# Converting float64 weights on chip: a whole-number significand times a power of two made by ScalarE, five VectorE operations per piece in place of six

## The chip, the cores and the metric

The kernel runs on one core of a Trainium2 chip. The time is the device time of one execution in microseconds (us), the median of several runs. A core has a matrix engine (TensorE, in the profile PE, with its weight loads as PEld), a vector engine (VectorE, DVE), a scalar engine for functions and copies (ScalarE, ACT), a general one (GpSimd, POOL) and one that mostly issues transfers (SyncE, SP). Each has its own instruction stream; they meet at semaphores.

## What is computed

```python
# attention part: q, k, v are (4, 8, 768, 64) float32
for t in range(S):
    state = gamma[None, :, None, None] * state + np.einsum('bhd,bhe->bhde', k[:, :, t], v[:, :, t])
    y[:, :, t] = scale * np.einsum('bhd,bhde->bhe', q[:, :, t], state)
x = y.transpose(0, 2, 1, 3).reshape(B * S, H * D)        # (3072, 512)
# feed-forward part: w_in (512, 2048), w_out (2048, 512)
h = x @ w_in
sp = np.maximum(h, 0.0) + np.log1p(np.exp(-np.abs(h)))
g = h * erf(sp)
return (g @ w_out).astype(np.float32)                    # (3072, 512)
```

The two weight matrices come out of the set-up as float64 (a float32 array times a float64 scalar). The kernel reads them as 64-bit words and makes float32 of them on the chip. This conversion is what is changed.

## The kernel before

The recurrence is done in 24 blocks of 128 positions (`j`), each with transposes, a masked product of q and k, a product with v and a running state. Blocks 0 to 3 feed the first 512 rows (groups `g` = 0 to 3, plain products); the later rows use a scheme of seven products of half size, which needs sums of weight quarters.

The weights come in 16 pieces of 1 MiB (two transfers of 512 KB each). A piece is 128 partitions by 1024 numbers of two 32-bit words, `lo` and `hi`. It lands in one of four spare areas of the weight tiles `w_in_sb` and `w_out_sb`; further spare areas hold intermediate results (`low`, and `tops`, of which there are two, used in turn).

```python
spare = [
    x[:, s, 4:7].rearrange("p a b c -> p (a b c)") for s, x in
    ((0, w_out_sb), (1, w_out_sb), (1, w_in_sb), (0, w_in_sb))
]
raws = [x[:, : 2 * CE].bitcast(I64) for x in spare]        # place 2 lies in w_in_sb
low = spare[0][:, 2 * CE :].bitcast(U32)
tops = [x[:, 2 * CE :].bitcast(U32) for x in spare[1:3]]
pieces = [("in", 0), ("in", 1)]                            # then in 2, in 3, out 0, out 1, in 4, ...
place = [n % 4 if n < n_p - 4 else (n - n_p + 4) % 3 for n in range(n_p)]

def conversion(n):                                         # L192 on; cut
    nc.vector.tensor_scalar(top, hi, 3, 0x3FFFFFF8, ...)             # L205: 8 times the magnitude bits
    yield
    nc.vector.scalar_tensor_tensor(top, hi, 0xC0000000, top, ...)    # L209: sign and top bit back
    yield
    nc.scalar.activation(square, square, AF.Square)                  # L213, in place on hi
    yield
    nc.vector.tensor_scalar(low, top, 0xFF800000, None, ...)         # L215: power of two of it
    yield
    nc.vector.scalar_tensor_tensor(lowf, lo, 2.0**-52, lowf, ...)    # L217: low word, scaled
    yield
    nc.vector.tensor_tensor(lowf, topf, lowf, op=ALU.add)            # L219
    yield
    nc.vector.scalar_tensor_tensor(to, square..., F64_LEAST**2, lowf..., op0=ALU.is_ge, op1=ALU.mult)  # L221
    done.add(pieces[n])
    load_pieces_after(n)      # load the next piece of this place
    yield
```

Each engine runs its instructions in the order in which the program emits them. The steps of the conversion are woven in between other work: `pace(x)` adds `x` to a budget and emits one step of `weights()` for every whole unit of it; `need(what)` emits steps until a piece is there.

```python
def weights():                                             # L250
    for n in range(2):
        for i, _ in enumerate(conversion(n)):
            if i != 2:
                yield
    before = iter(())
    for n in range(2, n_p):
        now = conversion(n)
        for _ in range(2):
            next(now)
            yield
        if n > 2:
            next(before)
            yield
        next(now)
        for _ in before:
            yield
        before = now
        ...

def ret_scale(j):       # VectorE, L397: k and q of a block times their decays
    nc.vector.tensor_tensor(KQ[j], KQ[j], by, op=ALU.mult)
    pace(-1.1)
def ret_transpose(j):   # TensorE L412, then ScalarE copies kT and qT, L418
    ...
    pace(1)
def ret_scores(j):      # TensorE L425
    ...
    pace(1)
def ret_mask(j):        # VectorE L437, two per block: am = scores times mask
    ...
    pace(-1.2)
def ret_out(j):         # TensorE L460, L465 (needs am), L474; ScalarE copies xT, L479
    ...
    pace(2.5)
def ret_loads(j):
    if j == 0 or j == JPC:
        load(j + 3)                                        # k, q, v of a block
    if j in (1, 2):
        load_piece(j + 1)

for j in range(n_first):                                   # blocks 0 to 3
    S_(j); M(j); K_(j + 1); O_(j); T(j + 1)                # scores, mask, scale, out, transpose (cut)
    ret_loads(j)
    pace(1)
    A(j)                                                   # state, VectorE L493/L495
```

After that come, for each group, `hidden` (products with w_in, TensorE L541, copied to `h` by ScalarE, L544), `gate` (Softplus and Erf on ScalarE, L506 and L511), `gated` (two products on VectorE, L530) and `project` (products with w_out, L554); from group 4 on `hidden_part` (L611) and `project_part` (L683). `load_pieces_after` holds the loads back until block 3 is emitted.

Of the kernel before, what the change touches and what calls it, by code (L numbers as in the profile page):

```python
# [12 lines left out]
F32 = mybir.dt.float32  # L13
U32 = mybir.dt.uint32
I64 = mybir.dt.int64
AF = mybir.ActivationFunctionType
ALU = mybir.AluOpType
PSUM = bass.MemoryType.PSUM

P = 128  # L20
# [18 lines left out]
}  # L39


F64_LEAST = float(np.array(897 << 20, np.uint32).view(np.float32))


@with_exitstack
def kernel(
# [13 lines left out]
    nc = tc.nc  # L60
# [14 lines left out]
    const = ctx.enter_context(tc.tile_pool(name="const", bufs=1))  # L75
# [52 lines left out]
    def w_out_of(ft):  # L128
# [5 lines left out]
    CE = 2 * d_model  # L134
    spare = [
        x[:, s, 4:7].rearrange("p a b c -> p (a b c)") for s, x in
        ((0, w_out_sb), (1, w_out_sb), (1, w_in_sb), (0, w_in_sb))
    ]
    raws = [x[:, : 2 * CE].bitcast(I64) for x in spare]
    low = spare[0][:, 2 * CE :].bitcast(U32)  # L140
    tops = [x[:, 2 * CE :].bitcast(U32) for x in spare[1:3]]
    pieces = [("in", 0), ("in", 1)]
    for n in range(4):
        if n < 3:
# [2 lines left out]
    n_p = len(pieces)  # L147
# [3 lines left out]
    def load_piece(n):  # L151
        which, i = pieces[n]
        w = raws[place[n]]
        if which == "in":
            for r in range(2):
                nc.sync.dma_start(
                    w[r * D : (r + 1) * D].rearrange("p (g f) -> p g f", g=n_k),
                    w_in[r * DH : (r + 1) * DH, i * 2 * P : (i + 1) * 2 * P].rearrange(
                        "(g p) f -> p g f", p=D
                    ),  # L160
                )
        else:
            for d in range(2):
                nc.sync.dma_start(
                    w.rearrange("p (d f c) -> p d f c", d=2, f=2)[:, d],
                    w_out[i * 2 * P : (i + 1) * 2 * P, d * DH : (d + 1) * DH].rearrange(
                        "(f p) c -> p f c", p=P
                    ),
                )
# [18 lines left out]
    def conversion(n):  # L188

        which, i = pieces[n]  # L192
        words = raws[place[n]].bitcast(U32).rearrange("p (n w) -> p n w", w=2)
        lo, hi = words[:, :, 0], words[:, :, 1]
        square = hi.bitcast(F32)
        half, s, at = i // 4, i % 4 // 2, i % 2
        if which == "in":
            to = w_in_sb[:, s, 2 * half : 2 * half + 2, :, at * 2 * P : (at + 1) * 2 * P]
            form, sizes = "p (d k f) -> p d k f", dict(d=2, k=2)
        else:  # L200
            to = w_out_sb[:, s, 2 * half : 2 * half + 2, at * 2 : at * 2 + 2, :]
            form, sizes = "p (d f c) -> p d f c", dict(d=2, f=2)
        top = tops[n % 2]
        topf, lowf = top.bitcast(F32), low.bitcast(F32)
        nc.vector.tensor_scalar(  # L205
            top, hi, 3, 0x3FFFFFF8, op0=ALU.logical_shift_left, op1=ALU.bitwise_and
        )
        yield
        nc.vector.scalar_tensor_tensor(  # L209
            top, hi, 0xC0000000, top, op0=ALU.bitwise_and, op1=ALU.bitwise_or  # L210
        )
        yield
        nc.scalar.activation(square, square, AF.Square)  # L213
        yield
        nc.vector.tensor_scalar(low, top, 0xFF800000, None, op0=ALU.bitwise_and)  # L215
        yield
        nc.vector.scalar_tensor_tensor(lowf, lo, 2.0**-52, lowf, op0=ALU.mult, op1=ALU.mult)  # L217
        yield
        nc.vector.tensor_tensor(lowf, topf, lowf, op=ALU.add)  # L219
        yield  # L220
        nc.vector.scalar_tensor_tensor(  # L221
            to,
            square.rearrange(form, **sizes),
            F64_LEAST**2,
            lowf.rearrange(form, **sizes),
            op0=ALU.is_ge,
            op1=ALU.mult,
        )
        done.add(pieces[n])
        load_pieces_after(n)  # L230
        yield

    def sums(which, s):

        if which == "in":
            assert all(("hidden", 2 * FG + s * FG + u) in done for u in range(FG))
            x = {name: w_in_sb[:, s, at] for name, at in IN.items()}
            of = (("S1", "21", "22", 1), ("S2", "S1", "11", 0), ("S3", "11", "21", 0), ("S4", "12", "S2", 0))
        else:
            assert ("project", s) in done  # L240
            x = {name: w_out_sb[:, s, at] for name, at in OUT.items()}
            of = (("T1", "12", "11", 0), ("T2", "22", "T1", 0), ("T3", "22", "12", 0), ("T4", "21", "T2", 0))
        for to, a, b, plus in of:
            nc.vector.tensor_tensor(x[to], x[a], x[b], op=ALU.add if plus else ALU.subtract)
            yield
        done.add(("sums " + which, s))
# [3 lines left out]
    def weights():  # L250


        for n in range(2):
            for i, _ in enumerate(conversion(n)):
                if i != 2:
                    yield
        before = iter(())
        for n in range(2, n_p):
            now = conversion(n)
            for _ in range(2):  # L260
                next(now)
                yield
            if n > 2:
                next(before)
                yield
            next(now)
            for _ in before:
                yield
            before = now
            if pieces[n - 1] == ("out", 5):  # L270
                yield from sums("in", 0)
        yield from before

    def later_sums():
        for which, n in (("in", 1), ("out", 0), ("out", 1)):
            yield from sums(which, n)

    weight_steps = weights()
    last_steps = later_sums()
    room = 0.0  # L280
# [9 lines left out]
    def need(*what):  # L290
        nonlocal room
        while what not in done:
            if next(weight_steps, done) is done:
                next(last_steps)
            room -= 1

    ident = const.tile([P, P], F32, name="ident")
    make_identity(nc, ident)
    nc.scalar.dma_start(d_k, decay_k)
# [3 lines left out]
    for s in range(2):  # L303
# [9 lines left out]
        out=causal, in_=causal, compare_op=ALU.is_ge, fill=0.0,  # L313
# [607 lines left out]
```

## Time and profile before

| what | value |
|---|---|
| time, median of 3 runs | 714.78 us (713.53 to 715.28) |
| span of the profiled execution | 711.6 us |
| TensorE busy | 697.9 us, 98% |
| VectorE busy | 399.4 us, 56%, 548 instructions |
| ScalarE busy | 257.0 us, 36%, 289 instructions |
| HBM read, written | 39.86 MB, 6.29 MB |
| chain of work that ended last | TensorE 95%, ScalarE 2%, DMA 2%, VectorE 1% |

A line of the profile in order of time has the start, the duration, the engine, the source line (L205 is line 205 of the kernel), the operation and its output and inputs by tile, and in brackets the idle time before it with what ended it. The source lines of the kernel after differ from those of the kernel before, as some lines are gone. Busy time of an engine is no measure of what it costs: only what the chain of waits runs through sets the end. The groups of the conversion in the kernel before, by line (count, busy time, mean duration), summed over tiles:

| line | engine | count | mean |
|---|---|---|---|
| L205, L215 | VectorE, one source | 16 each | 0.69 us |
| L209, L217, L219, L221 | VectorE, two sources | 16 each | 1.22 to 1.23 us |
| L213 | ScalarE, Square | 16 | 1.17 us |

### The profile page before, as it was taken

The page shows a single profiled execution, that of the slowest core. Times are in us where ns is not written, and L with a number is a line of the kernel's source. Part 1 is how long each engine was busy: PE and PEld are TensorE (multiplying, and loading weights), DVE is VectorE, ACT ScalarE, POOL GpSimd, SP SyncE. Part 2 cuts the span into 40 slices and gives each one's busy share as a digit, 9 for nine tenths or more (in the row PEclk, how much of TensorE's full clock was granted, in tenths as well). Part 3 has the DMA queues.
Part 4 walks back from the last instruction along what each step waited for, and adds up shares of the span by engine and source line. Part 5 has one row for each costly group of instructions (what it writes and reads, how often), then busy time and mean ns, then how long its engine had stood idle before and what let it go on. Part 6 is the DMA issues. An engine that isn't in the chain of part 4 may idle for free.

```text
span 711.6 us, 12107 instructions
## 1 busy us (share of the span) xinstructions
PE 697.9 (98%) x5132; PEld 592.4 (83%) x5132; DVE 399.4 (56%) x548; ACT 257.0 (36%) x289; POOL 5.2 (1%) x18
## 2 busy tenths in 40 slices
PE   6899999999999999999999999999999999999998
PEld 6644444486999999999999999989999999999997
DVE  3899999984863563554454544544553464243234
ACT  2345653525144143242341441442432423414431
POOL 1000000010000000000000000000000000000000
PEclk9899999999999999999999999999999999999999
DMA  9999743212321233211222313130221210000000
GB/s 187 208 243 229 183 136 119 38 23 40 100 40 33 61 64 53 56 35 27 64 40 42 69 35 60 45 59 13 47 71 33 42 48 1 2 31 1 1 30 29
DMA packets 147205, 46.96 MB, mean 66 GB/s; under 512 B 135760, under 2 KB 136016, under 8 KB 147152
## 3 DMA queue, kind: packets, MB, share of 16 engines
q1 hardware_dynamic: 143600, 45.40, 29.2%
q10 hardware_dynamic: 3552, 0.80, 0.7%
q8 instruction: 40, 0.66, 0.4%
q14 instruction: 13, 0.11, 0.1%
HBM read 39.86 MB, written 6.29 MB: 65 GB/s over the span
## 4 chain that ended last, share of the span: by engine, by line
PE 95%; ACT 2%; DMA 2%; DVE 1%; SPq 0%; issue 0%; ACTq 0%; DVEq 0%
PE hp L611 35%; PE o L683 34%; PE o L554 8%; PE hp L541 7%; PE r L465 3%; PE hp L425 3%; PE r L460 2%; DMA kq<-in_k_dram 2%; PE r L474 1%; PE r L425 1%; PE r L412 1%; ACT qT L418 0%; PE hp L465 0%; DVE am L437 0%; ACT e L506 0%
## 5 line engine op out<-in xcount | busy, mean ns | idle before, releaser
L611 PE MATMUL hp<-xs,w_in_sb 128*128 128x128 f32 x1280 | 149.8, 275 | 0.0
L611 PEld LDWEIGHTS hp<-xs,w_in_sb 128*128 128x128 f32 x1280 | 147.8, 192 | 1.6 <-issue 0.5
L683 PE MATMUL o<-w_out_sb,h 128*128 128x256 f32 x640 | 141.7, 379 | 0.0
L683 PEld LDWEIGHTS o<-w_out_sb,h 128*128 128x128 f32 x640 | 121.6, 190 | 16.5
L611 PE MATMUL hp<-xT,w_in_sb 128*128 128x128 f32 x960 | 113.7, 275 | 0.0
L611 PEld LDWEIGHTS hp<-xT,w_in_sb 128*128 128x128 f32 x960 | 111.9, 192 | 1.9 <-issue 1.0
L683 PE MATMUL o<-w_out_sb,e 128*128 128x256 f32 x480 | 112.1, 383 | 0.0
L530 DVE TENSOR_TENSOR e<-h,e 128x1024 f32<-128x1024 f32 x42 | 49.6, 1222 | 101.6 <-ACT e L511 101.6
L683 PEld LDWEIGHTS o<-w_out_sb,e 128*128 128x128 f32 x480 | 88.2, 190 | 12.5 <-PE r L465 0.2
L506 ACT ACT_TABLE_LOAD x24 | 30.8, 1283 | 79.1 <-issue 69.6
L541 PE MATMUL hp<-xT,w_in_sb 128*128 128x512 f32 x128 | 56.9, 596 | 0.5 <-ACT xT L479 0.5
L636 DVE TENSOR_TENSOR h<-h,hp 128x512 f32<-128x512 f32 x20 | 13.8, 688 | 75.3 <-PE hp L611 75.3
L541 PEld LDWEIGHTS hp<-xT,w_in_sb 128*128 128x128 f32 x128 | 23.8, 190 | 28.4 <-issue 27.4
L511 ACT ACTIVATE e<-e 128x2048 f32<-128x2048 f32 (+1 forms) x23 | 42.1, 1835 | 0.2
L506 ACT ACTIVATE e<-h 128x2048 f32<-128x2048 f32 x22 | 42.0, 1910 | 0.2
L479 ACT COPY xT<-r 128x256 f32<-128x256 f32 x44 | 14.4, 375 | 73.7 <-PE r L474 65.0
L624 DVE TENSOR_TENSOR h<-h,hp 128x512 f32<-128x512 f32 x20 | 13.8, 688 | 36.3 <-PE hp L611 36.2
L634 ACT COPY h<-hp 128x512 f32<-128x512 f32 x20 | 11.7, 586 | 60.3 <-PE hp L611 60.3
L629 ACT COPY h<-hp 128x512 f32<-128x512 f32 x20 | 11.7, 586 | 57.9 <-PE hp L611 57.9
L627 ACT COPY h<-hp 128x512 f32<-128x512 f32 x20 | 11.7, 586 | 55.3 <-PE hp L611 55.3
L511 ACT ACT_TABLE_LOAD x24 | 30.8, 1283 | 0.4
L631 DVE TENSOR_TENSOR h<-h,hp 128x512 f32<-128x512 f32 x20 | 13.7, 687 | 28.1 <-ACT h L629 28.1
(103 smaller groups left out, 678.5 us busy)
## 6 DMA issues: line engine op xcount, KB each, us to landing
w_out_sb<-in_moe_w_out_dram SPq DMA_DIRECT2D x14, 512.0 KB, 5.2
kq<-in_k_dram SPq DMA_DIRECT2D x24, 256.0 KB, 3.4
v<-in_v_dram SPq DMA_DIRECT2D x24, 256.0 KB, 3.3
w_in_sb<-in_moe_w_in_dram SPq DMA_DIRECT2D x12, 512.0 KB, 7.1
out_dram<-r SPq DMA_DIRECT2D x23, 256.0 KB, 2.5
kq<-in_q_dram SPq DMA_DIRECT2D x256, 16.0 KB, 1.8
kb<-in_k_dram SPq DMA_DIRECT2D x256, 16.0 KB, 1.7
w_out_sb<-in_moe_w_in_dram SPq DMA_DIRECT2D x4, 512.0 KB, 9.1
```

The lines of the kernel that those rows point to most:

```text
L425: nc.tensor.matmul(pp[s][:, hp, :], KT[j][s * D : (s + 1) * D, hp, :], QT[j][s * D : (s + 1) * D, hp, :], start=True, stop=True,)
L460: nc.tensor.matmul(place(h), state[own, u, :], QT[j][own, u, :], start=(h % 4 < 2), stop=False, skip_group_check=True,)
L465: nc.tensor.matmul(place(h), V[j][:, h, :], AM[j][:, h % 2, h // 2, :], start=(not c and h % 4 < 2), stop=True, skip_group_check=True,)
L479: nc.scalar.copy(XC[m][:, r::2, i * C : (i + 1) * C], pp[r][:, :2, :])
L506: nc.scalar.activation(E[g], HS[g], AF.Softplus)
L511: nc.scalar.activation(E[g][:, half], E[g][:, half], AF.Erf)
L530: nc.vector.tensor_tensor(E[g][:, half], HS[g][:, half], E[g][:, half], op=ALU.mult)
L541: nc.tensor.matmul(p, w_in_of(ft, kk), XC[0][:, kk, :], start=(kk == 0), stop=(kk == n_k - 1))
L554: nc.tensor.matmul(O[0][tt].rearrange("p (d c) -> p d c", d=2), E[g][:, u * TCH + tt * P : u * TCH + (tt + 1) * P], w_out_of(ft), start=(f ...
L611: nc.tensor.matmul(bank[:, u, :], w_in_sb[:, s, IN[a], kk, u * P : (u + 1) * P], XS[m][b][:, kk, :], start=(p in (1, 2, 5) and u == 0 and ...
L624: nc.vector.tensor_tensor(h["11"], h["11"], flat, op=ALU.add)
L683: nc.tensor.matmul(O[m][i][:, half, :], G[g][a][:, u * P : (u + 1) * P], w_out_sb[:, s, OUT[b], u, :], start=i not in started, stop=(s == ...
```

## The change

The number is built otherwise: the significand as a whole number (the 20 upper bits with the leading one, times 2^32, plus the low word), and the power of two from the exponent bits by one ScalarE operation, a Relu of 8 times the bits less a constant, which also makes zero of what is too small for float32. The product of both is the number. This takes five VectorE operations per piece in place of six. The buffer of a piece is free after the fourth of them. The weaving is changed with it: the first step of each piece from the third on is emitted ahead of all the rest of the piece before it, and the separate loop over the first two pieces is gone.

```diff
-F64_LEAST = float(np.array(897 << 20, np.uint32).view(np.float32))
+BELOW = 1023 - 127
...
-        nc.vector.tensor_scalar(
-            top, hi, 3, 0x3FFFFFF8, op0=ALU.logical_shift_left, op1=ALU.bitwise_and
-        )
-        yield
-        nc.vector.scalar_tensor_tensor(
-            top, hi, 0xC0000000, top, op0=ALU.bitwise_and, op1=ALU.bitwise_or
-        )
-        yield
-        nc.scalar.activation(square, square, AF.Square)
-        yield
-        nc.vector.tensor_scalar(low, top, 0xFF800000, None, op0=ALU.bitwise_and)
-        yield
-        nc.vector.scalar_tensor_tensor(lowf, lo, 2.0**-52, lowf, op0=ALU.mult, op1=ALU.mult)
-        yield
-        nc.vector.tensor_tensor(lowf, topf, lowf, op=ALU.add)
-        yield
-        nc.vector.scalar_tensor_tensor(to, square, F64_LEAST**2, lowf, op0=ALU.is_ge, op1=ALU.mult)
-        done.add(pieces[n])
-        load_pieces_after(n)
-        yield
+        power = powers[n % 2]
+        nc.vector.tensor_scalar(power, hi, 0x7FF00000, None, op0=ALU.bitwise_and)           # L203
+        nc.scalar.activation(power, power, AF.Relu, bias=below, scale=8.0)                  # L204
+        yield
+        nc.vector.tensor_scalar(                                                            # L206
+            number, hi, 0xFFFFF, 1 << 20, op0=ALU.bitwise_and, op1=ALU.bitwise_or
+        )
+        yield
+        numberf = number.bitcast(F32)
+        nc.vector.scalar_tensor_tensor(numberf, number, 2.0**32, lo, op0=ALU.mult, op1=ALU.add)   # L211
+        yield
+        nc.vector.scalar_tensor_tensor(                                                     # L213
+            power, hi, 1 << 31, power, op0=ALU.bitwise_and, op1=ALU.bitwise_or
+        )
+        load_pieces_after(n)
+        yield
+        nc.vector.scalar_tensor_tensor(to, numberf, 2.0**-52, power, op0=ALU.mult, op1=ALU.mult)  # L218
+        done.add(pieces[n])
+        yield
...
     def weights():
-        for n in range(2):
-            for i, _ in enumerate(conversion(n)):
-                if i != 2:
-                    yield
         before = iter(())
-        for n in range(2, n_p):
+        for n in range(n_p):
             now = conversion(n)
-            for _ in range(2):
+            if n > 1:
                 next(now)
                 yield
-            if n > 2:
-                next(before)
-                yield
-            next(now)
             for _ in before:
                 yield
             before = now
...
+    below = const.tile([P, 1], F32, name="below")
+    nc.gpsimd.memset(below, -float(BELOW << 23))
```

(The operands of the last operation are shown without their rearrangement, and line numbers of the changed kernel are added.)

More of the change, by code (lines that the diff above doesn't have):

```diff
@@ L139 @@
     raws = [x[:, : 2 * CE].bitcast(I64) for x in spare]
-    low = spare[0][:, 2 * CE :].bitcast(U32)
-    tops = [x[:, 2 * CE :].bitcast(U32) for x in spare[1:3]]
+    number = spare[0][:, 2 * CE :].bitcast(U32)
+    powers = [x[:, 2 * CE :].bitcast(U32) for x in spare[1:3]]
     pieces = [("in", 0), ("in", 1)]
@@ L194, in conversion @@
         lo, hi = words[:, :, 0], words[:, :, 1]
-        square = hi.bitcast(F32)
         half, s, at = i // 4, i % 4 // 2, i % 2
@@ L202, in conversion @@
             form, sizes = "p (d f c) -> p d f c", dict(d=2, f=2)
-        top = tops[n % 2]
-        topf, lowf = top.bitcast(F32), low.bitcast(F32)
+        power = powers[n % 2]
+        nc.vector.tensor_scalar(power, hi, 0x7FF00000, None, op0=ALU.bitwise_and)
+        nc.scalar.activation(power, power, AF.Relu, bias=below, scale=8.0)
+        yield
         nc.vector.tensor_scalar(
-            top, hi, 3, 0x3FFFFFF8, op0=ALU.logical_shift_left, op1=ALU.bitwise_and
+            number, hi, 0xFFFFF, 1 << 20, op0=ALU.bitwise_and, op1=ALU.bitwise_or
         )
         yield
+        numberf = number.bitcast(F32)
+        nc.vector.scalar_tensor_tensor(numberf, number, 2.0**32, lo, op0=ALU.mult, op1=ALU.add)
+        yield
         nc.vector.scalar_tensor_tensor(
-            top, hi, 0xC0000000, top, op0=ALU.bitwise_and, op1=ALU.bitwise_or
+            power, hi, 1 << 31, power, op0=ALU.bitwise_and, op1=ALU.bitwise_or
         )
-        yield
-        nc.scalar.activation(square, square, AF.Square)
-        yield
-        nc.vector.tensor_scalar(low, top, 0xFF800000, None, op0=ALU.bitwise_and)
-        yield
-        nc.vector.scalar_tensor_tensor(lowf, lo, 2.0**-52, lowf, op0=ALU.mult, op1=ALU.mult)
-        yield
-        nc.vector.tensor_tensor(lowf, topf, lowf, op=ALU.add)
+        load_pieces_after(n)
         yield
@@ L222, in conversion @@
             to,
[L223 to L226, printed above, removed]
+            numberf.rearrange(form, **sizes),
+            2.0**-52,
+            power.bitcast(F32).rearrange(form, **sizes),
+            op0=ALU.mult,
             op1=ALU.mult,
@@ L269, in weights @@
             before = now
-            if pieces[n - 1] == ("out", 5):
+            if n and pieces[n - 1] == ("out", 5):
                 yield from sums("in", 0)
```

## The prediction

> **What bounds the kernel now.** I read the page's totals first, then the busy time of each engine by stage, because the conversion of the weights runs only in the first part. By stage (busy us of each engine, granted TensorE clock, share of the DMA engines, GB/s):
>
> ```profile
> PE 697.9 (98%) x5132; PEld 592.4 (83%) x5132; DVE 399.4 (56%) x548; ACT 257.0 (36%) x289; POOL 5.2 (1%) x18
> ...
> 0.00:35.00 35.00, 26.70 (x294) 22.82 (x296) 21.00 (x31) 9.88 (x18) 2.15 (x13) 0.85 1.05 197
> 35.00:60.00 25.00, 23.01 (x84) 10.70 (x80) 24.24 (x25) 13.95 (x17) 0.00 (x0) 1.00 1.05 232
> 60.00:100.00 40.00, 39.85 (x196) 20.19 (x197) 39.10 (x41) 18.56 (x23) 0.00 (x0) 1.00 0.76 183
> 100.00:145.00 45.00, 45.00 (x118) 20.85 (x117) 43.89 (x46) 21.29 (x19) 0.00 (x0) 1.00 0.33 88
> 145.00:711.60 566.60, 563.37 (x4449) 517.86 (x4448) 271.21 (x409) 193.30 (x215) 3.06 (x5) 1.00 0.19 41
> ```
>
> TensorE is the bound: from 60 us on it is idle for 0.15 us up to 145 and for 3.2 us at the very end, where the last outputs leave. VectorE is nearly full from 35 to 145 us (24.24 of 25, 39.10 of 40, 43.89 of 45), but always just ahead of TensorE. So work taken off VectorE there can't shorten the span. All that could be won is TensorE's idle time before 60 us: 8.3 us before 35 and 2.0 us after. In those first microseconds the chain of work goes through the transfer of the second block of k (11.04 us of it), and then around the loop TensorE, ScalarE copies, masks on VectorE, for each block of the recurrence. The DMA engines are full there (share 1.05). What matters is therefore in which order VectorE takes its work between 14 and 37 us, and whether its operands have landed. VectorE in order of time (start, duration, line):
>
> ```profile
> 24.39 1.23 DVE L219 TENSOR_TENSOR w_out_sb<-w_out_sb 128x1024 f32<-128x1024 f32 x1
> 25.53 0.42 DVE L493 TENSOR_TENSOR state<-state,r 128x256 f32<-128x256 f32 x1
> 25.86 1.22 DVE L221 SCALAR_TENSOR_TENSOR w_in_sb<-w_out_sb 128x1024 f32<-128x1024 f32 x1
> 27.69 0.69 DVE L437 TENSOR_TENSOR am<-r,causal 128x512 f32<-128x512 f32 x1 [0.61 <-PE hp L425]
> 28.30 0.68 DVE L437 TENSOR_TENSOR am<-hp,causal 128x512 f32<-128x512 f32 x1
> ...
> 33.37 0.69 DVE L437 TENSOR_TENSOR am<-r,causal 128x512 f32<-128x512 f32 x1 [0.46 <-PE hp L425]
> ...
> 38.29 0.69 DVE L205 TENSOR_SCALAR w_out_sb<-w_in_sb 128x1024 uint32<-128x1024 uint32 x1
> ```
>
> L221 ends piece 0; the masks L437 at 27.69 and 33.37 are those of blocks 2 and 3; the first operation that touches piece 2 (L205 with w_in_sb as its source) comes only at 38.29. When did piece 2 land? Its two transfers are the first two of the four that the sync queue issues at 25.29 (1.86 us for the two in a narrower look, so the second starts at about 26.5). Sync queue, then the landing times of transfers issued in the slices 25 to 25.8 and 26.6 to 27.1 us (last number, median us from issue):
>
> ```profile
> 18.69 6.55 SPq L114 DMA_DIRECT2D v<-in_v_dram  x1
> 25.29 1.86 SPq L156 DMA_DIRECT2D w_in_sb<-in_moe_w_in_dram  x2
> ...
> w_in_sb<-in_moe_w_in_dram SPq DMA_DIRECT2D x1, 512.0 KB, 6.5
> ...
> w_in_sb<-in_moe_w_in_dram SPq DMA_DIRECT2D x1, 512.0 KB, 7.7
> ```
>
> 25.29 + 6.5 = 31.8 and 26.5 + 7.7 = 34.2: piece 2 is whole at 34.2 us. Before, nothing asks for it until 38.29.
>
> [...] The trace agrees, in that no instruction of VectorE starts ahead of its place in the program. [...] idle for 3.35 us before 16.07, and then
>
> ```profile
> 12.00:16.00 4.00, 0.73 (x22) 0.59 (x18) 1.25 (x2) 0.65 (x2) 0.00 (x0) 0.82 1.37 218
> 16.00:20.00 4.00, 3.25 (x20) 2.88 (x22) 2.83 (x4) 2.19 (x3) 0.00 (x0) 0.50 1.24 217
> 20.00:24.00 4.00, 4.00 (x50) 3.35 (x50) 3.20 (x4) 0.00 (x0) 0.00 (x0) 0.50 1.10 203
> 24.00:28.00 4.00, 3.22 (x52) 2.75 (x48) 3.36 (x5) 1.72 (x4) 0.00 (x0) 0.90 1.04 189
> ```
>
> half clock (0.50) for about 10 us[...]. [...] the trace has 0.69 us for a one-source operation on 128x1024 and 1.22 to 1.23 us for a two-source one, with the strided words too. [...] Relu in place of Square should bring no table load; the built kernel has as many loads as before.
>
> **The change part by part.**
> 1. VectorE's work. Before, a piece has two operations of 0.69 and four of 1.23 us, 6.3 us; after, two of 0.69 (mask, whole number) and three of 1.23 us, 5.1 us. Over 16 pieces 16 x 1.225 = 19.6 us leave VectorE (399 to about 380). By the stage table that lies beside TensorE: worth 0, at most the 0.32 us by which the scaling of block 4 is late for its transpose (TensorE waits at 54.27).
> 2. ScalarE: 16 Squares of 1.17 us become 16 Relus of the same size. No change in sum, but the places change (point 5).
> 3. The order on VectorE. The first operation of piece n+1 is now emitted ahead of *all* of piece n, already for the first pieces (the loop over pieces 0 and 1 is gone, and `if n > 1` starts piece 2 before piece 1). With two steps fewer in piece 0, its end and the mask L203 of **piece 2** fall before block 2's masks. The built kernel has on VectorE: piece 0's last operation, the addition to the state, L203 on piece 2 (waiting for both transfers), the two masks of block 2, the scaling of block 3, L203 on piece 1. So L203 stands at about 25.9 us and waits until 34.2. Nothing in the change moves those transfers earlier: until then the sync queue holds the same transfers with waits on the same things. L203 ends at 34.9; block 2's masks start at 34.85 instead of 27.69, **7.2 us late**, and TensorE stands still from 28.2 to 35.6 us.
> 4. The clock. 7.3 us of idle TensorE are more than the 3.35 that halved it before. The loop of block 1, all at 0.50, takes 8.44 us from transpose to transpose (16.07 to 24.51), that of block 2 5.79 us (24.51 to 30.30): factor 1.46. From the end of the wait, TensorE has 8.1 us of such work until the hidden products (28.43 to 36.52). If the half clock lasts until 43 to 46 us, 7.4 to 10.7 us of it lie on this work and cost 0.31 of their length: **2.3 to 3.3 us**. The hidden products then start at 46 to 47 us instead of 36.52, 9.5 to 10.5 us late, and from there TensorE is the bound, so the delay reaches the end.
> 5. ScalarE's order after the first gate: a Relu (1.17 us) now stands between the copy of the hidden product and the copies of kT and qT of block 4; before, a Square came only after them. TensorE already waits there 1.35 us for qT (at 60.15), so **+1.2 us**. In block 5 the same shift meets a reserve: qT ends at 89.4, and its product starts at 92.07. Block 1 too has a Relu ahead of its copies, some 0.2 us, but that is swallowed by the wait until 34.2.
> 6. Reload: a piece's buffer is free one operation earlier (L213 is the last to read it). The later loads come sooner, TensorE's delay gives the DMA 10 us, so no new wait for pieces 3 to 15 is expected: 0.
>
> Sum: 7.2 + 2.8 + 1.2 - 0.3 = 10.9 us; 714.8 + 10.9 = **725.7 us**, 1.5% slower.
>
> **The rivals.**
> - Relief: VectorE was the bound of the conversion, and the first 150 us become shorter by some of the 19.6 us. For it: VectorE at 97% in that stretch. Against it: TensorE without gaps there. It would give 712 to 715.
> - Nothing: piece 2 lands before it is asked for, if the wait for an earlier transfer that keeps the queue at 18.69 (6.55 us) ends sooner; landing at 30 would leave 3 us of delay and perhaps no half clock: 718 to 720.
> - Starved conversion: in its quicker rhythm VectorE asks for 1 MiB every 5 us, which at 217 GB/s (the rate from 20 to 40 us) takes 4.8 us without the 0.75 MiB of each k, q, v block. Masks and gating products queued behind a missing piece then hold TensorE again. Against it: the share of the DMA engines is 0.76 from 60 to 100 us. It would add 2 to 6 us: 728 to 732.
>
> **Range and chances.** The stall is the surest term, since the order is built in and the landing is measured; its size moves with the landing by 1 or 2 us, and the half clock is uncertain by 2 us. That gives 719 to 730 for 8 of 10. 2% slower is 729.1, which needs the third rival or a longer half clock: 0.15. Faster by 2% means 700.5 us, which TensorE's 697.9 us of busy time all but shut out: 0.01. Within 2%: 0.84.
>
> **What would show it.** In the changed kernel's trace: L203 with w_in_sb as its source idle some 8 us before it, put down to the transfer from moe_w_in, starting near 34 us; block 2's masks right behind; granted clock near 0.5 between 33 and 43; the first hidden product at 46 to 47 us; VectorE's sum near 380; the wait for qT of block 4 near 2.5 us; TensorE without gaps from 75 us on. I am wrong if L203 on piece 2 finds its data, or if TensorE has gaps after 75 us.

## The result, and the profile after

The changed kernel takes 725.62 us (median of 4 runs, 724.60 to 726.78), the kernel before 714.15 us (4 runs, 713.20 to 715.28) in the same session: a ratio of 1.016, with a 95% interval of 1.0135 to 1.0186. The change makes the kernel 1.6% slower. The span of the profiled execution is 722.8 us against 711.6, 11.2 us more.

The busy time of each engine in the kernel after, from the totals of the page:

```profile
PE 699.8 (97%) x5132; PEld 594.2 (82%) x5132; DVE 379.7 (53%) x532; ACT 256.7 (36%) x289; POOL 5.2 (1%) x19
```

VectorE (DVE) has 16 instructions and 19.7 us less to do, as planned: 379.7 in place of 399.4 us. ScalarE has 49 table loads in either kernel. The same stages as before, with busy us of each engine (TensorE first, VectorE third), granted TensorE clock, share of the DMA engines, GB/s:

```profile
0.00:35.00 35.00, 20.72 (x212) 18.13 (x212) 13.21 (x21) 7.01 (x13) 2.19 (x14) 0.86 1.08 198
35.00:60.00 25.00, 22.41 (x139) 12.88 (x140) 23.11 (x28) 9.20 (x15) 0.00 (x0) 0.92 0.77 178
60.00:100.00 40.00, 37.08 (x152) 18.83 (x151) 35.38 (x38) 23.63 (x24) 0.00 (x0) 0.96 1.02 242
100.00:145.00 45.00, 45.00 (x147) 20.58 (x146) 38.58 (x41) 20.73 (x23) 0.00 (x0) 1.00 0.29 71
```

In the first 35 us TensorE was busy for 26.70 us before and for 20.72 now, and VectorE for 21.00 before and 13.21 now: both stand still together. From 100 us on TensorE has no idle time, as before, and VectorE has 6.4 us to spare where it had 1.1. That spare time brings nothing. All that the change costs is spent before 77 us. VectorE of the kernel after, in order of time:

```profile
25.39 1.23 DVE L218 SCALAR_TENSOR_TENSOR w_in_sb<-w_out_sb 128x1024 f32<-128x1024 f32 x1
26.54 0.42 DVE L483 TENSOR_TENSOR state<-state,r 128x256 f32<-128x256 f32 x1
34.65 0.69 DVE L203 TENSOR_SCALAR w_out_sb<-w_in_sb 128x1024 uint32<-128x1024 uint32 x1 [7.69 <-DMA w_in_sb<-in_moe_w_in_dram]
35.26 0.68 DVE L427 TENSOR_TENSOR am<-r,causal 128x512 f32<-128x512 f32 x1
```

L218 ends piece 0, L483 adds to the state, and then VectorE waits 7.69 us for the transfer of piece 2 before it can run L203, the first step of that piece. The masks of block 2 (L427) are next in its queue: 35.26 us, where the kernel before has them at 27.69. Nothing in those masks needs piece 2, and TensorE is done with the scores they read at 29.11 us, where its own wait begins. TensorE of the same kernel:

```profile
36.00 0.69 PE L455 MATMUL r<-am,v 128*64 128x128 f32 x4 [6.89 <-DVE am L427]
...
45.17 17.43 PE L531 MATMUL hp<-xT,w_in_sb 128*128 128x512 f32 x40 [0.47 <-ACT xT L469]
...
69.84 2.08 PE L415 MATMUL r<-qT,kT 64*128 64x128 f32 x16 [2.92 <-ACT qT L408]
71.84 4.33 PE L531 MATMUL hp<-xT,w_in_sb 128*128 128x512 f32 x8
76.10 0.67 PE L450 MATMUL r<-qT,state 64*64 64x128 f32 x16
```

There are two stops. The first (6.89 us at the masked product) is that of the masks. The second is at the scores of block 4: 2.92 us for qT, against 1.35 before. There the Relu L204 has come between two copies of ScalarE that follow each other in the kernel before. ScalarE of the kernel after, then of the kernel before:

```profile
67.21 0.57 ACT L534 COPY h<-hp 128x512 f32<-128x512 f32 x1
67.67 1.15 ACT L204 ACTIVATE w_out_sb<-w_out_sb,below 128x1024 uint32<-128x1024 uint32 x1
68.72 0.57 ACT L408 COPY kT<-r 128x512 f32<-128x512 f32 x1
```

```profile
58.56 0.57 ACT L544 COPY h<-hp 128x512 f32<-128x512 f32 x1
59.02 0.59 ACT L418 COPY kT<-r 128x512 f32<-128x512 f32 x1
```

The work behind each of the two stops starts at half clock (0.50). The granted clock (the number after POOL's busy time) in four stretches of the kernel after:

```profile
32.00:36.00 4.00, 0.00 (x1) 0.01 (x1) 1.35 (x3) 0.62 (x1) 0.00 (x0) 0.52 1.05 217
36.00:39.00 3.00, 3.00 (x33) 2.58 (x34) 2.88 (x4) 0.52 (x1) 0.00 (x0) 0.50 1.05 218
39.00:42.00 3.00, 2.22 (x28) 1.86 (x32) 1.56 (x2) 2.77 (x5) 0.00 (x0) 1.00 0.57 211
...
70.00:73.00 3.00, 3.00 (x18) 2.26 (x19) 1.06 (x2) 1.32 (x2) 0.00 (x0) 0.50 1.05 384
```

In the second of these slices (36 to 39 us) and in the last (70 to 73) TensorE is fully busy at 0.50. The 16 score products L415 take 2.08 us in place of 1.16, and the eight hidden products behind them 4.33 in place of 3.70.

In the kernel before the masks of block 2 stand at 27.69. TensorE of the kernel before at the three points that follow:

```profile
36.52 17.43 PE L541 MATMUL hp<-xT,w_in_sb 128*128 128x512 f32 x40 [0.47 <-ACT xT L479]
...
60.15 1.16 PE L425 MATMUL r<-qT,kT 64*128 64x128 f32 x16 [1.35 <-ACT qT L418]
...
64.88 0.67 PE L460 MATMUL r<-qT,state 64*64 64x128 f32 x16
```

So the 11.2 us come out as a sum:

| from one point to the next | delay so far | added here | cause |
|---|---|---|---|
| masks of block 2: 35.26 for 27.69 | 7.57 | 7.57 | wait for piece 2 |
| first hidden product: 45.17 for 36.52 | 8.65 | 1.08 | half clock from 36 to 39 us |
| scores of block 4: 69.84 for 60.15 | 9.69 | 1.04 | copies of kT and qT later |
| product with the state: 76.10 for 64.88 | 11.22 | 1.53 | half clock from 70 to 73 us |

After that the two kernels run in step to the end.

### The profile page after: what moved, and what is told of

It is laid out like the page before. It is cut to its first block, busy times and chain, and to the rows that moved or that the text cites. A ratio compares the mean times of both kernels' runs of the same rounds, so it can differ in the third digit from the quotient of the medians.

```text
span 722.8 us, 12069 instructions
## 1 busy us (share of the span) xinstructions
PE 699.8 (97%) x5132; PEld 594.2 (82%) x5132; DVE 379.7 (53%) x532; ACT 256.7 (36%) x289; POOL 5.2 (1%) x19
## 4 chain that ended last, share of the span: by engine, by line
PE 93%; DMA 3%; ACT 2%; SPq 1%; DVE 1%; issue 0%; DVEq 0%
PE hp L601 35%; PE o L673 34%; PE o L544 8%; PE hp L531 7%; PE r L455 3%; PE hp L415 3%; DMA kq<-in_q_dram 2%; PE r L450 1%; PE r L464 1%; DMA w_in_sb<-in_moe_w_in_dram 1%; SPq L114 1%; PE r L415 1%; DMA kq<-in_k_dram 0%; PE r L402 0%; DVE am L427 0%; ACT e L496 0%
## 5 line engine op out<-in xcount | busy, mean ns | idle before, releaser
L626 DVE TENSOR_TENSOR h<-h,hp 128x512 f32<-128x512 f32 x20 | 13.7, 687 | 75.3 <-PE hp L601 75.3
L614 DVE TENSOR_TENSOR h<-h,hp 128x512 f32<-128x512 f32 x20 | 13.8, 688 | 55.3 <-PE hp L601 55.3
L455 PE MATMUL r<-am,v 128*64 128x128 f32 x352 | 26.2, 286 | 8.9 <-DVE am L427 8.9
L624 ACT COPY h<-hp 128x512 f32<-128x512 f32 x20 | 11.7, 585 | 60.3 <-PE hp L601 60.3
```

What stands on the lines that cost most here:

```text
L455: nc.tensor.matmul(place(h), V[j][:, h, :], AM[j][:, h % 2, h // 2, :], start=(not c and h % 4 < 2), stop=True, skip_group_check=True,)
L614: nc.vector.tensor_tensor(h["11"], h["11"], flat, op=ALU.add)
L626: nc.vector.tensor_tensor(h["12"], h["12"], flat, op=ALU.add)
```

## The experiments

Each time is a median; each ratio is to the kernel before in the same session (medians 713.47 to 713.70 us), with its 95% interval.

**The order alone undone.** The first step of a piece is emitted ahead of the rest of the piece before it only from piece 4 on.

```diff
-            if n > 1:
+            if n > 3:
                 next(now)
                 yield
```

> The kernel after, but pieces 2 and 3 are not begun ahead of the piece before them (the first step of a piece goes ahead only from piece 4 on). Theory A (the loss is the wait of VectorE for the landing of piece 2, with the half clock that follows it): the wait of 7.7 us before piece 2's mask and the half clock from 33 to 39 us go; what stays is the wait for qT of block 4 (Relu of piece 6 ahead of its copies) with the half clock after it, 2.6 us over before: 716.7 us (716 to 718). Rival B (the new operations or the quicker rhythm on the transfers cost the time, wherever piece 2 stands): it stays near 725. Rival C (relief of VectorE counts once the wait is gone): below 713.

Measured: 714.73 us, 1.0022 [1.0012, 1.0031]. Of the 11.5 us between the two kernels, about 10 go with this one condition. The masks of block 2 run at 26.95 us, 0.74 us ahead of those of the kernel before, and the hidden products start at 35.79. The result is better than I expected, because I had counted on the later copies and the half clock behind them in full. VectorE, then TensorE of this kernel:

```profile
26.19 0.69 DVE L203 TENSOR_SCALAR w_in_sb<-w_out_sb 128x1024 uint32<-128x1024 uint32 x1
26.95 0.69 DVE L427 TENSOR_TENSOR am<-r,causal 128x512 f32<-128x512 f32 x1
```

```profile
35.79 17.43 PE L531 MATMUL hp<-xT,w_in_sb 128*128 128x512 f32 x40 [0.47 <-ACT xT L469]
...
54.47 1.09 PE L402 MATMUL r<-ident,kq 128*128 128x128 f32 x8 [1.25 <-DVE kq L387]
...
60.44 1.16 PE L415 MATMUL r<-qT,kT 64*128 64x128 f32 x16 [1.44 <-ACT qT L408]
```

The scores come 24.65 us after the first hidden product (35.79 to 60.44), as in the kernel after (24.67) and not as before (23.63): the later copies still cost 1.0 us. But the idle time is in two halves here, 1.25 us at the transposes (the scaling stood behind the first step of piece 4, which waited 1.89 us for its transfer) and 1.44 us at the scores. Neither is followed by a half clock: the transposes take 1.09 us, as at 54.27 in the kernel before, and from 60 to 80 us the granted clock is 1.00. So the fourth row of the table falls away.

**The landing alone taken away.** The order stays, but the first steps of pieces 2 and 3 read words that lie on the chip already: those of pieces 0 and 1. What it leaves out: the exponents of pieces 2 and 3 never reach the output.

```diff
-        nc.vector.tensor_scalar(power, hi, 0x7FF00000, None, ...)
+        first = hi
+        if n in (2, 3):
+            first = <hi of raws[place[n - 2]]>
+        nc.vector.tensor_scalar(power, first, 0x7FF00000, None, ...)
```

> The kernel after in its own order, but the first mask of pieces 2 and 3 reads the words of pieces 0 and 1, which have landed (so the exponents of pieces 2 and 3 are left out, and the output is not the reference's). Theory A: the order alone costs nothing, only the wait for the landing does; the mask runs at about 26.5 us without a wait and the time is that of the run with the order undone, 716.7 us (716 to 718). If the place in the order costs by itself (VectorE's work before the masks of block 2), the time stays above 719.

Measured: 722.81 us, 1.0132 [1.0118, 1.0146], a miss. The masks of block 2 now ran without a wait, but the place of piece 1 was being filled with piece 5 when piece 3's first step came to read it. VectorE of this kernel:

```profile
46.24 0.70 DVE L206 TENSOR_SCALAR w_in_sb<-w_out_sb 128x1024 uint32<-128x1024 uint32 x1 [7.11 <-DMA w_out_sb<-in_moe_w_out_dram]
```

It (L206 is the first step here) waited 7.11 us for that transfer, and the scaling of block 4 with it, so that TensorE stood 5.02 us at 62.56. I had moved the wait to another transfer, and the kernel became nearly as slow again. With piece 3's step reading piece 2 instead (piece 2's still reads piece 0; the same exponents are left out):

```diff
-            first = <hi of raws[place[n - 2]]>
+            first = <hi of raws[0 if n == 2 else 2]>
```

> The kernel after in its own order, but the first mask of piece 2 reads the words of piece 0 and that of piece 3 the words of piece 2, which have landed by then (the exponents of pieces 2 and 3 are left out, so the output is not the reference's). The earlier form of this run read for piece 3 a place that was already being filled again, and so waited 7.1 us for piece 5. Theory A: only the wait for the landing costs, not the place in the order: no wait before block 2's masks, 715 to 717.5 us. If the place costs by itself, above 719.

Measured: 714.95 us, 1.0025 [1.0015, 1.0034]. Every instruction stands in the order of the kernel after, only the wait for the transfer is gone, and so is the loss, but for the 1.0 us of the later copies (36.13 to 60.78 is 24.65 us again). VectorE of this kernel, with the first step of piece 2 and the masks of block 2:

```profile
26.38 0.69 DVE L206 TENSOR_SCALAR w_out_sb<-w_out_sb 128x1024 uint32<-128x1024 uint32 x1
27.30 0.69 DVE L430 TENSOR_TENSOR am<-r,causal 128x512 f32<-128x512 f32 x1 [0.23 <-PE hp L418]
```

So here the new place in the queue costs nothing by itself; the wait in that place does (7.69 us in the kernel after).

**The weave alone, with the arithmetic of before.** The six operations of before, with the ScalarE operation sharing a step with the next one, in the order of the kernel after. In a first form the Square kept a step of its own, which makes seven steps per piece:

```diff
-        for n in range(2):
-            for i, _ in enumerate(conversion(n)):
-                if i != 2:
-                    yield
-        for n in range(2, n_p):
+        for n in range(n_p):
             now = conversion(n)
-            for _ in range(2):
+            if n > 1:
                 next(now)
                 yield
-            if n > 2:
-                next(before)
-                yield
-            next(now)
```

> The kernel before with its six operations, but with the weaving of after (each piece from the third on begun ahead of the piece before, no separate loop for the first two). As six operations take more steps, the first operation on piece 2 comes later here, behind the masks of block 2 and before those of block 3. Theory A: it waits until piece 2 has landed (34.2 to 34.7 us), the masks of block 3 start near 36.4 instead of 33.4 us: 3 us over before, up to 4.5 with a half clock: 717 to 719 us. Rival B (the new operations cost it): 714, as before.

Measured: 770.61 us, 1.0803 [1.0787, 1.0820]. This form tells nothing of the order. A budget meant for six steps per piece falls behind with seven: the sums of weight quarters, which the program emits by a count of their own, take areas that aren't converted yet (this is read from the program, not shown by a run). So this run doesn't compute the whole function, and TensorE waits for the weights themselves, for instance 7.65 us for L221 at 85.52. With six steps:

```diff
         nc.scalar.activation(square, square, AF.Square)
-        yield
         nc.vector.tensor_scalar(low, top, 0xFF800000, None, ...)
```

> The kernel before with its six operations in six steps, and the weaving of after. (The earlier form gave the Square a step of its own, so the conversion fell behind the sums that reuse its areas.) The first operation on piece 2 now stands behind the scaling of block 3, at 30.0 us, ahead of the masks of block 3. Theory A: it waits until 34.2 us or a little later, the masks of block 3 start near 37 instead of 33.4 us: 3.6 us over before, with a half clock up to 4.7: 717 to 719 us. Rival B (the new operations cost it): 714.

Measured: 724.09 us, 1.0138 [1.0122, 1.0154]. The kernel before, with nothing changed but the order of its steps, is nearly as slow as the kernel after. I had expected some 4 us. VectorE, then TensorE of this kernel:

```profile
35.02 0.69 DVE L205 TENSOR_SCALAR w_out_sb<-w_in_sb 128x1024 uint32<-128x1024 uint32 x1 [5.85 <-DMA w_in_sb<-in_moe_w_in_dram]
```

```profile
36.70 0.47 PE L451 MATMUL r<-qT,state 64*64 64x128 f32 x1 [4.42 <-DVE state L484]
...
41.91 19.34 PE L532 MATMUL hp<-xT,w_in_sb 128*128 128x512 f32 x40 [0.47 <-ACT xT L470]
```

With six steps per piece the first step of piece 2 comes one block later, ahead of the state and masks of block 3. By then less of the wait is left (5.85 us), but the hidden products start 5.4 us late. The granted clock is 0.50 until 45.8 us, which reaches into them: these forty take 19.34 us in place of 17.43. The transposes of block 4 are at 62.54, 8.3 us late. Waits for masks further on, 0.57 us at 72.79 and 1.04 us at 106.41, are part of the rest up to the 10.4 us by which this kernel is slower.

**ScalarE's order alone.** The Relu of piece 6 is emitted one step later, so that the copies of kT and qT of block 4 come ahead of it.

```diff
-        nc.scalar.activation(power, power, AF.Relu, ...)
+        if not (n == 6):
+            nc.scalar.activation(power, power, AF.Relu, ...)
         yield
         nc.vector.tensor_scalar(number, ...)
+        if n == 6:
+            nc.scalar.activation(power, power, AF.Relu, ...)
```

> The kernel after, but the Relu of piece 6 is emitted one step later, so that it stands behind the copies of kT and qT of block 4 on ScalarE. The wait for piece 2 stays. Theory A: the wait for qT falls from 2.92 to about 1.8 us, the half clock after it goes, 2.6 us less than after: 723.0 us (722.2 to 723.8). If the copies wait for the gate's Softplus and Erf anyway and the Relu is hidden, it stays at 725.6.

Measured: 722.90 us, 1.0135 [1.0121, 1.0149], as expected. TensorE of this kernel:

```profile
45.91 17.43 PE L534 MATMUL hp<-xT,w_in_sb 128*128 128x512 f32 x40 [0.47 <-ACT xT L472]
...
69.54 1.16 PE L418 MATMUL r<-qT,kT 64*128 64x128 f32 x16 [1.89 <-ACT qT L411]
```

From 45.91 to 69.54 it is 23.63 us, to the hundredth as in the kernel before. The score products take 1.16 us again: behind 1.89 us of idle time the granted clock stayed at 1.00. So the third and the fourth row of the table, 2.57 us together, both hang on this one Relu. The profiled execution gains only 1.8 of them (721.0 us for 722.8), as its first half clock lasted until 41.1 us (39.0 in the kernel after) and cost 0.8 us more: 9.98 us from the first masked product to the first hidden product, where the kernel after takes 9.17.

**Both undone.** The two edits above together; the arithmetic with five operations stays.

```diff
-            if n > 1:
+            if n > 3:
 ...
+        if n == 6:
+            nc.scalar.activation(power, power, AF.Relu, ...)    # one step later, as above
```

> The kernel after with the order of pieces 2 and 3 undone and the Relu of piece 6 behind the copies of kT and qT of block 4. Theory A: both losses are gone and the 19.6 us that VectorE saves are worth nothing: 714.0 us (713.3 to 714.8), the ratio to before 1.000. Rival C (relief): 709 to 712.

Measured: 714.19 us, 1.0011 [1.0002, 1.0021]. (The profiled execution of this kernel was disturbed, 1853.6 us, so no line of it is shown.) With both losses out, 19.6 us less work on VectorE leave the time within 0.2% of what it was. This is the relief less what the quicker conversion loses by meeting transfers, as in the 1.89 us wait for piece 4 above; the two can't be told apart here.

**The load itself.** Is VectorE's work in that stretch free in both directions? To the last kernel, a second copy of the sign operation is added from piece 5 on, in the same step, so that the order of steps stays. The repeated operation changes no value.

```diff
-        nc.vector.scalar_tensor_tensor(power, hi, 1 << 31, power, ...)
+        for _ in range(2 if n >= 5 else 1):
+            nc.vector.scalar_tensor_tensor(power, hi, 1 << 31, power, ...)
```

> As the run with both losses undone, but from piece 5 on the operation that sets the sign is done twice (same result), 11 more operations of 1.23 us on VectorE, 13.5 us, so that it has about as much to do as before. Theory A: TensorE is the bound there, the time is the same within 0.5 us: 714.0. Rival C (VectorE's load counts in the conversion): 3 us or more longer.

Measured: 720.21 us, 1.0098 [1.0083, 1.0113]. This is a miss. VectorE, then TensorE of this kernel:

```profile
95.74 2.48 DVE L217 SCALAR_TENSOR_TENSOR w_out_sb<-w_in_sb,w_out_sb 128x1024 uint32<-128x1024 uint32 x2
...
100.72 1.28 DVE L431 TENSOR_TENSOR am<-r,causal 128x512 f32<-128x512 f32 x2
```

```profile
101.46 0.43 PE L454 MATMUL r<-qT,state 64*64 64x128 f32 x2 [2.78 <-DVE am L431]
```

The budget counts steps, not time. With longer steps the masks of block 5 stand behind more work, and TensorE waits 2.78 us for them, after 1.69 us at the transposes of block 4 and 1.66 us at the scores of block 5. So 11 more operations of 1.24 us, 13.6 us of VectorE, cost 6.0 us. It isn't the amount of work: VectorE is busy for 393.0 us here, and for 399.4 us in the kernel before, where TensorE waits 1.7 us in all from 40 us on. There a piece takes six steps, here five, of which one lasts 2.48 us.

**Fill the wait.** To see whether the half clock comes from the idle time, 56 products of the identity with itself are put between the scores of block 2 and its masked product, in the kernel after. Their output is used by nobody.

```diff
+        if j == 2:
+            keep_warm(56)
```

> The kernel after with 56 idle products of 128x128 on TensorE between the scores of block 2 and its output, some 6 us of the 7 in which it waits for the masks. Theory A with a half clock caused by idle time: the wait for piece 2 stays, the clock stays full from 33 to 39 us, and the products after it start 1.1 us earlier: 724.5 us (724 to 725). If the half clock has another cause, it stays at 725.6 or the idle products make it longer.

Measured: 727.01 us, 1.0186 [1.0173, 1.0200]. The time is a miss, the mechanism a hit. TensorE of this kernel:

```profile
26.88 12.77 PE L361 MATMUL o<-ident 128*128 128x128 f32 x112
...
47.89 17.43 PE L531 MATMUL hp<-xT,w_in_sb 128*128 128x512 f32 x40 [0.47 <-ACT xT L469]
...
72.56 1.16 PE L415 MATMUL r<-qT,kT 64*128 64x128 f32 x16 [2.92 <-ACT qT L408]
```

A product takes 0.228 us (12.77 / 56; each leaves two records), more than I had reckoned, and the filler runs to 39.65, more than 3 us after the first mask is there (35.75 to 36.43). But the granted clock stays at 1.00 from 28 to 44 us, and from the end of the filler to the first hidden product it is 8.2 us, where the kernel after needs 9.2 from the start of the masked product (36.00 to 45.17) and the kernel before 8.1. So the 1.08 us of the second row are the half clock, and with the wait filled there is none. At 72.56 the same wait of 2.92 us as in the kernel after was followed by a granted clock of 1.00 (72 to 76 us); why was not shown.

**Versions meant to beat both.** To the kernel with both losses undone, two conversion steps are emitted ahead of the fourth copy of a hidden product, so that the Relu of piece 5, too, comes ahead of the copies that TensorE waits for:

```diff
+        early_steps = 2 if (g, u) == (0, 3) else 0
+        pace(early_steps)
 ...
-        pace_around(3.4)
+        pace_around(3.4 - early_steps)
```

> As the run with both losses undone, and two steps of the conversion are emitted ahead of the fourth copy of the hidden product, so that the Relu of piece 5 runs before that copy and the first gate starts right after it. Theory A (only what stands on ScalarE ahead of qT of block 4 counts): the wait for qT of 1.35 us falls to about 0.2: 1.1 us less than the run with both losses undone, 712.9 us (712.2 to 713.6), the first version below the kernel before. If ScalarE's order there does not count: 714.0.

Measured: 714.14 us, 1.0014 [1.0004, 1.0024]. The wait at the scores of block 4 is gone, but VectorE asks for piece 10 2.79 us before it has landed (at 81.84), and the masks of block 5 behind it are late. So the first steps of pieces 4 and 10 are moved two steps back:

```diff
-            if n > 3:
-                next(now)
-                yield
-            for _ in before:
-                yield
+            ahead = {4: 2, 10: 2}.get(n, 0) if n > 3 else 9
+            for k in range(5):
+                if k == ahead:
+                    next(now)
+                    yield
+                if next(before, done) is not done:
+                    yield
```

> As the run with the first gate freed, and the first steps of pieces 4 and 10 are emitted two steps later, since in that run VectorE waits there for landings (about 2 and 2.8 us), which delays block 4's scaling (TensorE waits 1.15 us) and block 5's masks (0.8 us). Theory A with the third rival of the prediction (a piece asked for before it has landed holds the queue): both waits shrink, 1.5 us less than that run and clearly below the kernel before: ratio 0.997 to 0.999. If the gain is lost again elsewhere: 1.001 as before.

Measured: 713.75 us, 1.0000 [0.9992, 1.0009]. TensorE, then VectorE of this kernel:

```profile
69.14 13.90 PE L551 MATMUL o<-w_out_sb,e 128*128 128x512 f32 x32
...
96.52 0.66 PE L455 MATMUL r<-qT,state 64*64 64x128 f32 x14 [0.17 <-DVE am L432]
```

```profile
86.71 0.70 DVE L203 TENSOR_SCALAR w_in_sb<-w_in_sb 128x1024 uint32<-128x1024 uint32 x1 [1.90 <-DMA w_in_sb<-in_moe_w_in_dram]
```

The first products with w_out start at 69.14 us, 1.36 us ahead of the kernel before (70.50). At the state product of block 5 the lead is 0.27 us (96.52 for 96.79): now the next piece's first step waits 1.90 us for its transfer at 86.71, and the same masks come late. Both of these versions convert earlier and meet a transfer, for 2.79 and 1.90 us.

The last one adds 13 identity products between blocks 0 and 1 to this kernel, against the half clock that the kernel before has from 14.5 to 24.8 us:

```diff
+        if j == 0:
+            keep_warm(13)
```

> As the run just described, with 13 idle products (about 3 us) on TensorE between blocks 0 and 1, where it waits 3 us for the second block of k. The half clock from 16 to 24 us should go. The loop of block 1 is then 2.6 us shorter, but block 3's scaling has to wait for its k and q, which land near 28 us, so that about 1.1 us of it stays: ratio about 0.9985 of the run just described. If the clock at 16 us is not set by this idle time: no change.

Measured: 714.84 us, 1.0018 [1.0008, 1.0027]; no gain. The clock is at 1.00 up to 35 us, and block 1 takes 5.56 us from its transposes to those of block 2 (18.08 to 23.64) in place of the 7.45 of the kernel without filler. But the filler ends at 18.24, 2.2 us after the scaled operand of block 1 is ready (16.04); the masks of block 2 then wait for piece 1 (0.59 us), and the hidden products start at 36.20 as without filler (36.14). Later a transfer of q for block 4 lands late; VectorE and TensorE of this kernel:

```profile
54.77 1.22 DVE L392 TENSOR_TENSOR kq<-kq,kq_s 128x1024 f32<-128x1024 f32 x1 [1.95 <-DMA kq<-in_q_dram]
```

```profile
56.05 1.19 PE L407 MATMUL r<-ident,kq 128*128 128x128 f32 x8 [2.42 <-DVE kq L392]
57.03 5.25 PE L536 MATMUL hp<-xT,w_in_sb 128*128 128x512 f32 x8
```

It costs 2.42 us and a new half clock (0.50 from 56.9 to 60.3 us; 5.25 us for products of 3.60). Why q lands later there was not tried. None of the versions beats the kernel before.

## Why the prediction was right, and where its terms were off

The predicted 725.7 us and the measured 725.62 agree, and "within 2%" holds. The agreement of the sum is better than that of its terms, and in part it is luck: the first half clock cost 1.7 us less than predicted, and a second one, not foreseen, added 1.5 us.

| step | predicted | measured | shown by |
|---|---|---|---|
| 1 VectorE's relief | 0 to -0.3 | 0, net of new waits for transfers | both undone: 1.0011 |
| 3 mask L203 on piece 2 waits | +7.2 | +7.57 | order undone, landing taken away, weave alone |
| 4 half clock after it | +2.8 | +1.08 | filler |
| 5 Relu ahead of kT and qT | +1.2 | +1.04 | Relu of piece 6 later |
| second half clock | not foreseen | +1.53 | Relu of piece 6 later |
| 6 reload, pieces 3 to 15 | 0 | 0 in the kernel after | stages without gaps |
| sum | 10.9 | 11.2 | |

The measured terms are those of one execution of 724.60 us. The other three, of 724.90 to 726.78 us, have a lower mean clock (0.983 to 0.985, against 0.987), so the terms of the half clock vary from one execution to the next.

- Step 3 is right in place, cause and size. L203 started at 34.65 where 34.2 was predicted. Three runs show the cause from three sides: another order, another source for the same instruction, and the old arithmetic in the new order.
- Step 4 was mis-sized. I let the half clock run for 7 to 11 us from the end of the stop, after the 10 us of the kernel before. It began at 32.2 us, in the middle of the idle time, and ended at 39.0, so only 3.0 us of work lay on it. In the kernel before, too, the half clock began inside the stop, at 14.5 us, while the stop lasted until 16.07; slices of 4 us blur this. What ended each was not shown. "Granted clock near 0.5 between 33 and 43" holds only up to 39, and "first hidden product at 46 to 47" was 45.17.
- Step 5 has the right mechanism. The Relu pushes the copies by 1.05 us (from 67.67 to 68.72), and this shows at the scores as 1.04 in the profile of the kernel after and 1.02 in those of the undone order and of the landing taken away. The wait itself is 2.92 us, not the 2.5 foreseen, since TensorE gets there 0.5 us sooner relative to ScalarE: the transposes of block 4 no longer wait for their scaling. This is also why the -0.3 of step 1 didn't come: ScalarE's chain from the gate to the copies sets that point, not TensorE.
- What was missing: the half clock behind this wait of 2.92 us (0.50 from 69.7 to 73.1). I had applied step 4 to the long stop alone.
- Of the rivals, Relief falls with the run in which both losses are undone (1.0011) and with a TensorE that is never idle from 100 to 145 us, and Nothing with the 7.69 us wait of L203. Starved conversion isn't what slows the kernel after: VectorE waits once more for a transfer, 0.79 us at 90.95, where step 6 expected no new wait, but TensorE doesn't wait after 77 us. Yet the versions that convert earlier meet it: waits of 1.89 us for piece 4 (order undone), 2.79 us for piece 10 (the two steps ahead of the fourth copy) and 1.90 us at 86.71 (pieces 4 and 10 moved back).
- The working of step 1, "worth 0", is true of taking work away. I had taken it to hold for added work too when I expected the doubled operation to cost nothing, and it doesn't: 6.0 us.

The two terms that came out right, steps 3 and 5, rest on a waiting or running instruction holding up what stands behind it on its engine. In the trace of the kernel before, VectorE's 548 instructions and ScalarE's 289 come in the program's order of source lines. In the kernel after, VectorE starts nothing in the 7.69 us ahead of L203, though the scores that the masks behind it read are there at 29.11 us; and ScalarE copies kT at 68.72, behind the 1.15 us of L204, though the transposes that it reads end at 63.48.

## What to carry to other kernels

An instruction moved ahead in VectorE's queue brought its wait along: here one early 0.69 us operation, on data that the kernel before first touches at 38.29 us, waited 7.69 us and held up masks that had nothing to do with it. So before starting a step early, look up when its operand lands and what stands behind it in that queue. If an engine other than the bound gets less to do, look for what its work gave way to rather than for its busy time: keep the old order of the steps, change the arithmetic alone, and measure that first. When work is woven in by a count of steps, the length of a step is part of the schedule: here steps of 2.48 in place of 1.22 us moved the masks behind them, and TensorE waited 2.78 us.

## What the runs showed of the hardware

- The granted clock fell to 0.50 in or behind stops of TensorE, not behind each of them, and stayed there for 3.4 to 10.2 us. Read from half-microsecond slices (an edge inside a slice is an estimate from the mean clock of that slice):

| kernel | stop ahead, us | work starts again at | granted clock |
|---|---|---|---|
| before | 3.35 | 16.07 | 0.50 from 14.5 to 24.8 |
| after | 2.29 and 1.64 | 17.00 and 19.70 | 0.50 from 18.5 to 25.4 |
| after | 6.89 | 36.00 | 0.50 from 32.2 to 39.0 |
| after | 2.92 | 69.84 | 0.50 from 69.7 to 73.1 |
| weave alone | 4.42 | 36.70 | 0.50 from 35.5 to 45.8 |
| Relu of piece 6 later | 9.61 | 35.93 | 0.50 from 30.9 to 41.1 |
| last version | 2.42 | 56.05 | 0.50 from 56.9 to 60.3 |
| Relu of piece 6 later | 1.89 | 69.54 | 1.00 |
| filler | 2.92 | 72.56 | 1.00 |

The length of the stop alone doesn't tell what follows: of two stops of 2.92 us one was followed by 0.50 and one by 1.00. Nor does the time since the stop: behind the stop the half clock went on for 8.7 us in the kernel before (16.07 to 24.8) and for 3.0 us in the kernel after (36.00 to 39.0). What sets the beginning and the end was not shown.
- TensorE's lead on a late transfer gained nothing in one run, and cost. With the Relu of piece 6 moved, block 1 had no half clock (1.00 from 12 to 30.5 us), TensorE came earlier to the same wait and stood for 9.61 us in place of 6.89. The masked product started at 35.93 us in place of 36.00, and the half clock, 10.2 us in place of 6.8, cost the 0.8 us named above.
